# A planner that writes out the order of a fused attention and FFN kernel: DMA transposes dearer and limited in the plan, load costs set anew, and a new order for every engine

## The chip, the cores and the metric

The kernel runs on one core of a Trainium2 chip. A core has five engines that run side by side and wait for each other by semaphores: TensorE (PE in the profile; PEld is its weight load), VectorE (DVE), ScalarE (ACT), GpSimd (POOL) and SyncE (SP). The metric is the device time of one execution in microseconds. Three runs of the kernel before took 253.11 to 253.57 us, with a median of 253.48 us.

## The reference, cut to what matters

```python
B, H, S, D = 8, 8, 576, 64               # chunks of 64 positions: 9 in a batch entry, 72 in all
scores = scale * np.matmul(q_c, k_c.transpose(0, 1, 2, 4, 3))
scores = scores - np.max(scores, axis=-1, keepdims=True)
attn = np.exp(scores); attn = attn / (np.sum(attn, axis=-1, keepdims=True) + 1e-09)
out = np.matmul(attn, v_c)
x = out.transpose(0, 2, 1, 3).reshape(B * S, H * D)      # 4608 x 512
a, b = x @ w1, x @ w2                                    # w1, w2: 512 x 1024
y = (a * b @ w3) @ w_out                                 # w3: 1024 x 1024, w_out: 1024 x 512
```

Attention stays within a chunk of 64 positions and one head. All inputs and the output are float32; the kernel computes in bfloat16 with float32 sums.

## The kernel before, in words

**The work.** Two chunks (128 tokens) make a group; there are 36 groups, g0 to g35. Nine FFN tiles take four groups (512 tokens) each. The two last weights are multiplied into one first (`w3o` = w3 times w_out, `add_w3o`, L526).

For a group (`add_group`, L351) the steps are these. GpSimd loads q and k into a tile `raw` and casts them on the way (`load_qk`, L264). The tile is transposed: on TensorE for g0 to g11 (g0 to g3 from `quad` tiles of their own), and for g12 to g35 by a DMA transpose that SyncE issues (`qk_turn`, L409), into a tile `kqT`. Two copies on ACT or DVE (L235, L237) bring the q half into `qd`. TensorE makes the scores `p_sc` (L436; L387 for the quads); in what follows **S(g)** is this step. DVE and ACT make the softmax: maximum, subtraction, exponential, sum, reciprocal, product `an` (L441 to L463). `an` is transposed into `at`: on TensorE for g0 to g15 (L468), and for g16 to g35 by another DMA transpose on SyncE (`at_turn`, L415). TensorE multiplies `at` with `vd`, the loaded v (L479; L394 for the quads); this step is **V(g)**. A copy puts the result into `xt`.

An FFN tile (`add_tile`, L564) makes 8 pairs of blocks of four matmuls from `xt` with w1 and w2 (L576), an ACT copy and a DVE product for each pair (L235, L585), then four blocks of eight matmuls with `w3o` (L607), and copies their results out. SyncE stores them to `out`; the stores are queued after all loads of q and k.

**Queues.** All loads of q, k, v, w1, w2, w3 and the second half of w_out are issued by GpSimd into one queue (q0 in the profile), in the order of the list `LOADS` (L18) and then g by g. An issue waits for the landing of the load eight places ahead of it, and for a free tile. There are six `raw` tiles; one of g12 or later comes free when its DMA transpose has landed. SyncE's queue (q1) takes the first half of w_out together with ACT's (q10), then the DMA transposes, then the stores. There are four `kqT` tiles, six `at` tiles and three `vd` tiles (`BUFS`, L203). SyncE issues in order: an instruction that waits holds up all that are behind it.

**The order.** No loop nest sets the order. `Plan.run` (L70) simulates the five engines and the two DMA queues with a cost for every operation, and takes on each free engine the ready operation with the lowest key; the keys tell how far ahead of their use attention steps are to be made (`AHEAD`, L31). The sequence in which operations start in this simulation is the order in which they are emitted (L659 to L672), and so the order of each engine's instructions. The plan's times do not reach the chip in any other way, except through `fills`: where the plan sees TensorE idle early on, it puts in matmuls on zeros (L670) that nobody reads, one for each 0.25 us of the gap. In the plan a DMA sits in a ring; a transpose of q and k costs 1.75 us of the 16 DMA engines (L498) and one of `an` costs 0.88 us (L515). Both are counted as landed 3.5 us (`lag`) after their transfer is through, and the only limit on a ring is that it holds eight.

Of the kernel before, what the change touches and what calls it, by code (L numbers as in the profile page):

```python
# [29 lines left out]
LATE, LATE_A = 5, 2  # L30
AHEAD = [31, 28, 25, 19, 16]  # L31


class Op:


    def __init__(self, engines, cost, key, emit, after, takes, uses, lag, issue):
        self.engines = engines if isinstance(engines, tuple) else (engines,)
        self.cost, self.key, self.emit, self.lag, self.issue = cost, key, emit, lag, issue
        self.after, self.takes = list(after), takes  # L40
        self.users = {n: [] for n in takes}
        for taker, n in uses:
            taker.users[n].append(self)
        self.start = self.end = self.engine = None


class Plan:
# [12 lines left out]
    def add(self, engines, cost, key, emit, after=(), takes=(), uses=(), lag=0.1, issue=0.0):  # L60
        o = Op(engines, cost, key, emit, after, takes, uses, lag, issue)
# [8 lines left out]
    def run(self):  # L70
# [13 lines left out]
        rings, flown, reach = {"POOL": [], "SP": []}, 2.2, {"POOL": 1.6, "SP": 1.3}  # L84
# [25 lines left out]
        while left or any(rings.values()):  # L110
# [16 lines left out]
            for eng in free:  # L127
                if free[eng] > now or len(rings.get(eng, ())) + (eng == "POOL" and sum(x > now for x in landed)) >= self.RING:
                    continue
                pick = [o for o in (loads[:1] if eng == "POOL" else todo[eng]) if ready(o)]  # L130
                if not pick:
                    continue
                o = min(pick, key=lambda o: (o.key, o.place))
                for e in o.engines:
                    todo[e].remove(o)
                if eng == "POOL":
                    loads.pop(0)
                o.start, o.engine = now, eng
# [12 lines left out]
                if o.issue:  # L151
                    heapq.heappush(ends, rings[eng][-1][0])
                left -= 1
# [3 lines left out]
            after = ends[:1] + [flown + x[1] * len(h) for x in h]  # L157
            assert after or not left, "the plan is stuck"
# [5 lines left out]
def kernel(  # L164
# [91 lines left out]
    def load(cost, issue, emit, **kw):  # L256
        return plan.add("POOL", cost, 0, emit, lag=landing, issue=issue, **kw)
# [6 lines left out]
    def load_qk(g):  # L264
# [3 lines left out]
        for w, src in enumerate((q, k)):  # L268
            for r, b, c, n in parts:
# [4 lines left out]
                box["ops"].append(load(0.45 * n, 0.5 + 0.2 * n, emit, takes=() if box["ops"] else ("raw",)))  # L274
# [3 lines left out]
    def load_quad(n, y):  # L278
# [4 lines left out]
        for w, src in ((1, k), (0, q)):  # L283
            for t in range(2):
                for c, i0, i1 in parts:
# [8 lines left out]
                    box["ops"].append(load(0.088 * (i1 - i0), 0.5 + 0.02 * (i1 - i0), emit, takes=() if box["ops"] else ("rawq",)))  # L294

    def load_v(b, y0, y1):
        for t in range(2):
# [3 lines left out]
            o = load(1.0 * (y1 - y0), 0.5 + 0.335 * (y1 - y0), emit, takes=() if b in v_first else ("vd",),  # L301
# [5 lines left out]
    def load_w12(j0, j1):  # L307
        for dst, w in ((w1_sb, moe_w1), (w2_sb, moe_w2)):
            for t in range(2):
# [4 lines left out]
                o = load(0.36 * (j1 - j0), 0.62, emit)  # L314
# [10 lines left out]
    def load_wo(k0, k1):  # L325
        def emit(eng):
            nc.gpsimd.dma_start(wo_sb[:, k0:k1, :], moe_w_out.rearrange("(ko p) n -> p ko n", p=P)[:, k0:k1, :])
        wo_got.append([load(0.68 * (k1 - k0), 0.75, emit)])
# [22 lines left out]
    def add_group(g, kt, ks, ka, kv):  # L351
        box = {}
# [161 lines left out]
        if g in A_BY_DMA:  # L514
            ac = plan.add("SP", 0.88, ka, at_turn, after=(an,), takes=("at",), uses=[(an, "an")], lag=3.5, issue=1.3)  # L515
# [114 lines left out]
    made_ident, landing = None, 1.6  # L630
# [72 lines left out]
```

## Time and profile before

| what | value |
|---|---|
| median of three runs | 253.48 us (253.11 to 253.57) |
| the profiled execution, device time | 252.51 us |
| its span, first to last instruction | 250.7 us |
| busy: PE, DVE, ACT, POOL | 240.5, 174.1, 147.5, 100.1 us |
| matmuls, those on zeros included | 1798 |
| loads by GpSimd (q0) | 18.88 MB in 112016 packets |
| transposes and stores by SyncE (q1) | 18.88 MB in 41984 packets |

The profiled execution is 0.97 us below the median of the runs; 1.81 us of its own time lie around the span. A matmul's busy time covers its way through the array, so busy times of matmuls overlap; the distance between the starts of two matmuls tells what one costs. The chain of waits names, piece by piece, what the end of the span waited for; a DMA piece in it runs from the start of its issue to its landing. The timeline gives the start, the length and, in square brackets, the idle time before an instruction and what ended it.

### The profile page before, as it was taken

To read this page: it belongs to the slowest core of one execution; us is meant where nothing else is said; L and a number is where in the kernel's file an instruction comes from. 1 tells how busy PE (TensorE), PEld (TensorE's weight loads), DVE (VectorE), ACT (ScalarE), POOL (GpSimd) and SP (SyncE) were. 2 spreads that over 40 slices of the span, in tenths; PEclk is the share of its full clock that TensorE was granted. 3 is DMA by queue.
4 is the path that set the end of the run, shared out by engine and by line. 5 is a ranking of instruction groups with operands and counts; after the bars stand their busy time and mean duration, and the time that the engine had idled before them with its cause. 6 is when DMAs were issued, how large, how long until landed. Compare 5 with 4: busy or idle time off the path is not lost.

```text
span 250.7 us, 4768 instructions
## 1 busy us (share of the span) xinstructions
PE 240.5 (96%) x1798; PEld 122.3 (49%) x1798; DVE 174.1 (69%) x315; ACT 147.5 (59%) x250; POOL 100.1 (40%) x127
## 2 busy tenths in 40 slices
PE   7599999999999998999999989999999999999995
PEld 2356565456555454454444535454454444444443
DVE  6287879979879795988867978887898842222310
ACT  8666776667766786576558267655666433433222
POOL 8658579976695175357314631820000000000000
PEclk9999999999999999999999999999999999999999
DMA  7999999999999999999999999999999992121114
GB/s 200 173 205 174 175 180 175 166 145 126 135 113 144 150 155 137 139 138 149 133 154 156 136 156 156 142 156 152 137 171 256 388 356 106 43 84 42 44 42 167
DMA packets 154310, 38.58 MB, mean 154 GB/s; under 512 B 141232, under 2 KB 148272, under 8 KB 154288
## 3 DMA queue, kind: packets, MB, share of 16 engines
q0 software_dynamic: 112016, 18.88, 115.5%
q1 hardware_dynamic: 41984, 18.88, 43.2%
q10 hardware_dynamic: 288, 0.52, 0.5%
q8 instruction: 14, 0.23, 0.4%
q14 instruction: 8, 0.07, 0.1%
HBM read 38.80 MB, written 9.44 MB: 192 GB/s over the span
## 4 chain that ended last, share of the span: by engine, by line
PE 54%; DMA 32%; POOL 7%; issue 2%; ACT 2%; POOLq 0%
PE ffn L576 30%; PE ffn L607 20%; DMA kqT<-raw 16%; DMA w_sb<-in_moe_w_dram 10%; DMA raw<-in_k_dram 3%; DMA vd<-in_v_dram 3%; POOL w_sb L311 3%; PE p_av L479 2%; PE p_sc L436 2%; POOL raw L273 2%; ACT qd L235 2%; POOL rawq L292 1%; POOL vd L299 1%; PE ffn L407 1%; ACT rawq L235 0%
## 5 line engine op out<-in xcount | busy, mean ns | idle before, releaser
L576 PE MATMUL ffn<-xt,w_sb 128*128 128x512 bf16 x576 | 134.3, 379 | 0.0
L576 PEld LDWEIGHTS <-w_sb 128*128 128x128 bf16 x576 | 53.7, 98 | 58.2
L585 DVE TENSOR_TENSOR abT<-a_sb,ffn 128x512 bf16<-128x512 f32 x72 | 48.7, 679 | 35.1 <-PE ffn L576 33.1
L607 PE MATMUL ffn<-w3o_sb,abT 128*128 128x512 bf16 (+2 forms) x304 | 67.6, 368 | 0.0
L235 ACT COPY a_sb<-ffn 128x512 f32<-128x512 f32 x72 | 42.0, 583 | 29.5 <-PE ffn L576 27.9
L607 PEld LDWEIGHTS <-abT 128*128 128x128 bf16 x304 | 28.0, 98 | 29.7
L273 POOL DMA_DIRECT2D raw<-in_q_dram x36 | 30.5, 849 | 30.0 <-DMA vd<-in_v_dram 12.6
L273 POOL DMA_DIRECT2D raw<-in_k_dram x36 | 30.5, 851 | 26.3 <-DMA vd<-in_v_dram 15.6
L235 ACT COPY qd<-kqT 64x512 bf16<-64x512 bf16 x37 | 22.8, 615 | 16.4 <-DMA kqT<-raw 16.1
L441 DVE TENSOR_REDUCE nm<-p_sc 128x8 f32<-128x512 f32 x36 | 24.3, 674 | 5.1 <-PE p_sc L436 3.4
L457 DVE TENSOR_REDUCE ss<-e 128x8 f32<-128x520 bf16 x36 | 24.7, 687 | 4.3 <-ACT e L453 3.9
L235 ACT COPY o_sb<-ffn 128x512 f32<-128x512 f32 (+2 forms) x19 | 10.3, 540 | 28.8 <-PE ffn L607 28.8
L453 ACT ACTIVATE e<-sd 128x512 bf16<-128x512 f32 x36 | 22.8, 635 | 4.3 <-DVE sd L449 2.8
L463 DVE TENSOR_TENSOR an<-e,rs 128x512 bf16<-128x512 bf16 x36 | 24.6, 684 | 0.2
L449 DVE TENSOR_TENSOR sd<-p_sc,nm 128x512 f32<-128x512 f32 x32 | 21.8, 681 | 0.4
L299 POOL DMA_DIRECT2D vd<-in_v_dram x16 | 18.5, 1164 | 3.6 <-PE ffn L607 1.4
L235 ACT CAST xt<-p_av 128x512 bf16<-128x512 f32 x25 | 14.6, 585 | 8.1 <-PE p_av L479 6.8
L543 PE MATMUL ffn<-wo_sb,w3t 128*128 128x512 bf16 x64 | 16.3, 380 | 0.3 <-ACT w3t L235 0.2
L479 PEld LDWEIGHTS <-vd 128*128 128x128 bf16 x256 | 11.5, 98 | 8.5 <-DMA at<-an 1.4
L436 PEld LDWEIGHTS <-qd 128*128 128x128 bf16 x256 | 10.6, 98 | 7.5 <-ACT qd L235 3.8
L479 PE MATMUL p_av<-at,vd 128*128 128x64 bf16 x256 | 12.9, 193 | 0.6 <-DMA at<-an 0.3
L237 DVE CAST xt<-p_av 128x512 bf16<-128x512 f32 x11 | 7.6, 691 | 5.8 <-PE p_av L479 5.5
(55 smaller groups left out, 164.9 us busy)
## 6 DMA issues: line engine op xcount, KB each, us to landing
out_dram<-o_sb SPq DMA_DIRECT2D x19, 256.0 KB, 2.3
vd<-in_v_dram POOLq DMA_DIRECT2D x16, 288.0 KB, 13.8
raw<-in_q_dram POOLq DMA_DIRECT2D x28, 128.0 KB, 11.5
raw<-in_k_dram POOLq DMA_DIRECT2D x28, 128.0 KB, 10.4
w_sb<-in_moe_w_dram POOLq DMA_DIRECT2D x8, 256.0 KB, 8.2
w_sb<-in_moe_w_dram POOLq DMA_DIRECT2D x16, 128.0 KB, 5.1
out_dram<-w_sb SPq DMA_DIRECT2D x8, 256.0 KB, 4.0
out_dram<-wo_sb SPq DMA_DIRECT2D x4, 256.0 KB, 4.1
```

What stands on the lines that cost most here:

```text
L235: nc.scalar.copy(o, i)
L273: nc.gpsimd.dma_start(box["t"][r, w], src[b, :, c * C:(c + n) * C, :].rearrange("h p d -> p h d"))
L299: nc.gpsimd.dma_start(vds[b % len(vds)][halves[t], 2 * y0:2 * y1, :, t * D:(t + 1) * D].rearrange("p m c d -> p (m c) d"), v[b, NM * t + 2 ...
L441: nc.vector.tensor_reduce(nm[:, :, 0], box["sc"], axis=AX.X, op=ALU.max)
L449: nc.vector.tensor_sub(sd[:], box["sc"], box["nm"].to_broadcast([P, 8, C]))
L453: nc.scalar.activation(e[:, :, :C], box["sd"][:], ACT.Exp, scale=scale)
L457: nc.vector.reduce_sum(ss[:], box["e"][:], axis=AX.X)
L463: nc.vector.tensor_mul(an[:], box["e"][:, :, :C], box["rs"].to_broadcast([P, 8, C]))
L479: nc.tensor.matmul(t[:, m, cc, :], vds[b % len(vds)][:, m, c, :], box["at"][:, 2 * cc + y, u * C:(u + 1) * C], start=True, stop=True)
L576: nc.tensor.matmul(t[:, :w], wt[:, ki, j * P:(j + 1) * P], x[:, ki, :], start=(ki == 0), stop=(ki == KO - 1))
L585: nc.vector.tensor_mul(box["abT"][:, j, :w], box["as", j][:, :w], box["b", j][:, :w])
L607: nc.tensor.matmul(t[:, :x1 - x0], box["abT"][:, ki, tk * P:(tk + 1) * P], w3o_sb[:, ki, x0:x1], start=(ki == 0), stop=(ki == FO - 1))
```

## The change

The cost model inside the planner is changed, the head of the list of loads is put into another order, and with that the emitted order changes on all engines. No operation of the computation is added, dropped or reshaped.

- SyncE's queue is limited in the plan by the packets that it still holds (`queued`, `QUEUED`), with 2 units for a transpose of q and k, 1 for one of `an` and 0.25 for a store. At over 3.4 units the plan lets SyncE issue nothing.
- The transposes cost 2.0 and 0.95 us instead of 1.75 and 0.88, reach the queue 0.7 us later, and land 1.2 us instead of 3.5 us after their transfer.
- The DMA engines begin 3.5 us into the plan instead of 2.2, and the costs of all loads are set anew.
- In `LOADS` the identity matrix is made after the first quad and two slices of w3; the slices of w3 come in another order; the loads of g6 and g5 change places, as do slices of w1 and w2; v of batch entry 1 comes ahead of g8.

```diff
-LOADS = [('ident',), ('quad', 0, 0), ('w3', 4, 5), ('wo', 4, 8), ('w3', 2, 3), ('w3', 7, 8), ('quad', 0, 1), ('w3', 6,
-         7), ('qk', 4), ('w3', 1, 2), ('w3', 5, 6), ('v', 0, 0, 2), ('w3', 0, 1), ('w3', 3, 4), ('qk', 5), ('w12', 0,
-         2), ('qk', 6), ('w12', 2, 4), ('qk', 7), ('w12', 4, 6), ('w12', 6, 8), ('qk', 8), ('v', 1, 0, 2), ('qk', 9),
+LOADS = [('quad', 0, 0), ('w3', 5, 6), ('w3', 6, 7), ('ident',), ('wo', 4, 8), ('w3', 1, 2), ('quad', 0, 1), ('w3', 4,
+         5), ('w3', 0, 1), ('w3', 2, 3), ('v', 0, 0, 2), ('qk', 4), ('w3', 7, 8), ('w3', 3, 4), ('qk', 6), ('qk', 5),
+         ('w12', 0, 2), ('w12', 2, 4), ('w12', 6, 8), ('qk', 7), ('w12', 4, 6), ('v', 1, 0, 2), ('qk', 8), ('qk', 9),
          ('qk', 10)]
...
+FLOWN, QUEUED, LAG = 3.5, 3.4, 1.2
...
-        rings, flown, reach = {"POOL": [], "SP": []}, 2.2, {"POOL": 1.6, "SP": 1.3}
+        rings, flown, reach = {"POOL": [], "SP": []}, FLOWN, {"POOL": 1.6, "SP": 1.3}
...
+        def queued():
+            return sum(o.units * x / c for _, x, o, c in rings["SP"])
...
+                if eng == "SP" and queued() > QUEUED:
+                    continue
...
-                    rings[eng].append([free[eng] + reach[eng], cost, o])
+                    rings[eng].append([free[eng] + reach[eng] + o.reach, cost, o, cost])
...
-                box["ops"].append(load(0.45 * n, 0.5 + 0.2 * n, emit, takes=() if box["ops"] else ("raw",)))
+                box["ops"].append(load(0.445 * n, 0.5 + 0.2 * n, emit, takes=() if box["ops"] else ("raw",)))
...
-            o = load(1.0 * (y1 - y0), 0.5 + 0.335 * (y1 - y0), emit, takes=() if b in v_first else ("vd",),
+            o = load(1.07 * (y1 - y0), 0.5 + 0.335 * (y1 - y0), emit, takes=() if b in v_first else ("vd",),
...
-        o = load(1.42 * (k1 - k0), 0.75, emit)
+        o = load(1.29 * (k1 - k0), 0.75, emit)
...
-            tr = kc = plan.add("SP", 1.75, kt, qk_turn, after=got, takes=("kqT",), uses=[(got[0], "raw")], lag=3.5, issue=1.3)
+            tr = kc = plan.add("SP", 2.0, kt, qk_turn, after=got, takes=("kqT",), uses=[(got[0], "raw")],
+                               lag=LAG, issue=1.25, units=2, reach=0.7)
...
-            ac = plan.add("SP", 0.88, ka, at_turn, after=(an,), takes=("at",), uses=[(an, "an")], lag=3.5, issue=1.3)
+            ac = plan.add("SP", 0.95, ka, at_turn, after=(an,), takes=("at",), uses=[(an, "an")], lag=LAG, issue=1.25, units=1,
+                          reach=0.7)
...
-    made_ident, landing = None, 1.6
+    made_ident, landing = None, 1.1
```

More of the change, by code (lines that the diff above doesn't have):

```diff
@@ L30, with __init__ @@
 LATE, LATE_A = 5, 2
+FLOWN, QUEUED, LAG = 3.5, 3.4, 1.2
 AHEAD = [31, 28, 25, 19, 16]
 class Op:
-    def __init__(self, engines, cost, key, emit, after, takes, uses, lag, issue):
+    def __init__(self, engines, cost, key, emit, after, takes, uses, lag, issue, units, reach):
         self.engines = engines if isinstance(engines, tuple) else (engines,)
         self.cost, self.key, self.emit, self.lag, self.issue = cost, key, emit, lag, issue
+        self.units, self.reach = units, reach
         self.after, self.takes = list(after), takes
@@ L58, in __init__, with add @@
         self.turn = {n: [] for n in in_turn}
-    def add(self, engines, cost, key, emit, after=(), takes=(), uses=(), lag=0.1, issue=0.0):
-        o = Op(engines, cost, key, emit, after, takes, uses, lag, issue)
+    def add(self, engines, cost, key, emit, after=(), takes=(), uses=(), lag=0.1, issue=0.0, units=0.25,
+            reach=0.0):
+        o = Op(engines, cost, key, emit, after, takes, uses, lag, issue, units, reach)
         self.ops.append(o)
@@ L157, in run @@
             after = ends[:1] + [flown + x[1] * len(h) for x in h]
+            if queued() > QUEUED and rings["SP"][0] in h:
+                x = rings["SP"][0]
+                after.append(flown + min(x[1], (queued() - QUEUED) * x[3] / x[2].units) * len(h) + 1e-6)
             assert after or not left, "the plan is stuck"
@@ L293, in emit @@
                                             src[b, h:h + 2, c * C:(c + i1 - i0) * C, :].rearrange("h (p r) d -> p h (r d)", r=R))
-                    box["ops"].append(load(0.088 * (i1 - i0), 0.5 + 0.02 * (i1 - i0), emit, takes=() if box["ops"] else ("rawq",)))
+                    box["ops"].append(load(0.084 * (i1 - i0), 0.5 + 0.02 * (i1 - i0), emit, takes=() if box["ops"] else ("rawq",)))
     def load_v(b, y0, y1):
```

4 lines of the change are left out of this document (2 added, 2 removed).

## The prediction, as put on record

> **What bounds the kernel now.** I read the page first, then the busy time by stretches, the waits of PE, the chain of waits, and the timelines around the waits.
>
> ```profile
> span 250.7 us, 4768 instructions
> ...
> PE 240.5 (96%) x1798; PEld 122.3 (49%) x1798; DVE 174.1 (69%) x315; ACT 147.5 (59%) x250; POOL 100.1 (40%) x127
> ...
> PE   7599999999999998999999989999999999999995
> ...
> DMA  7999999999999999999999999999999992121114
> ```
>
> PE is busy all the way; only the first two slices and the last show much idle time. The DMA engines are just as full, but only up to about 205 us. So PE's own work is the floor, and what can be gained or lost is the time in which PE waits for a DMA.
>
> ```profile
> 150.93 0.23 PE p_av L479 x8
> 151.17 0.23 PE p_sc L436 x8
> 151.40 4.32 PE ffn L576 x20
> ...
> 56.56 0.45 PE ffn L407 x8
> ```
>
> These pieces of the chain of waits price a matmul from start to start: 216 ns for 512 columns (4.32 / 20), 56 for 128 (0.45 / 8), 29 for 64 (0.23 / 8). I use them for a bookkeeping. The **place** of an instruction is the sum of these prices over all real matmuls ahead of it in PE's order (the quads' 64 transposes, at 28 ns, stand ahead of all places below in both kernels, and fills on zeros are left out). The whole program sums to 229.74 us, before and after alike. The **lag** of an instruction is its start minus its place. Lag never falls; it rises where PE waits or runs a fill. The end of the span moves with the last lag, one for one.
>
> ```profile
> 37.35 1.03 PE L576 MATMUL ffn<-xt,w_sb 128*128 128x512 bf16 x4
> ...
> 73.85 0.40 PE L436 MATMUL p_sc<-kqT,qd 128*128 128x64 bf16 x8
> ...
> 84.20 0.41 PE L436 MATMUL p_sc<-kqT,qd 128*128 128x64 bf16 x8 [0.17 <-ACT qd L235]
> ...
> 100.06 0.41 PE L436 MATMUL p_sc<-kqT,qd 128*128 128x64 bf16 x8 [0.66 <-ACT qd L235]
> ...
> 127.67 0.41 PE L479 MATMUL p_av<-at,vd 128*128 128x64 bf16 x8 [0.35 <-DMA at<-an]
> ...
> 146.21 0.41 PE L436 MATMUL p_sc<-kqT,qd 128*128 128x64 bf16 x8 [1.19 <-ACT qd L235]
> ```
>
> In PE's order these are the first FFN block and S12, S14, S17, V19, S26. Their places in the kernel before, and so their lags:
>
> ```
>           place before  started  lag     place after
> first FFN    23.54        37.35  13.81      23.53
> S12          59.73        73.85  14.12      58.00
> S14          69.74        84.20  14.46      68.02
> S17          84.77       100.06  15.29      84.77
> V19         111.28       127.67  16.39     110.18
> S26         128.46       146.21  17.75     133.87
> ```
>
> So 13.81 us are lost in the start, 3.94 us at waits between S12 and S26 (0.34 up to S14, 0.83 up to S17, 1.10 up to V19, 1.36 at S26), and after S26 none: the stretch from 146.3 to 184 has PE busy for all of its 37.70 us.
>
> ```profile
> 146.30:184.00 37.70, 37.70 (x279) 18.93 (x279) 31.99 (x59) 24.24 (x43) 9.06 (x10) 1.00 1.76 150
> ```
>
> What PE waited for is in the chain and in ACT's timeline:
>
> ```profile
> 63.87 8.59 DMA raw<-in_k_dram
> 72.47 10.40 DMA kqT<-raw
> ...
> 135.71 9.18 DMA kqT<-raw
> ```
> ```profile
> 72.63 0.61 ACT L235 COPY qd<-kqT 64x512 bf16<-64x512 bf16 x1 [0.44 <-DMA kqT<-raw]
> ...
> 82.90 1.24 ACT L235 COPY qd<-kqT 64x512 bf16<-64x512 bf16 x2 [1.06 <-DMA kqT<-raw]
> ```
>
> S14 shows the pattern: the load of its k lands at 72.46 (63.87 + 8.59), its transpose is issued at 72.47 and lands at 82.87, two copies on ACT follow, and S14 starts at 84.20, 1.3 us after 82.90. S12's transpose landed by 72.63; in the kernel before one copy ran on ACT and one on DVE, and S12 was not held up.
>
> **The change part by part.** The costs, the limit on SyncE's queue and the lags are numbers inside the planner. They cost nothing on the chip; only the order and the fills do.
>
> *Start.* The identity matrix moves behind six loads, so GpSimd's first load is issued at 0.74 instead of 1.45, 0.71 us sooner.
>
> ```profile
> 0.74 0.20 POOL masks.py:197 MEMSET ident<- 128x128 bf16 x1 [0.29 <-POOLq L687]
> ...
> 1.45 1.56 POOL L292 DMA_DIRECT2D rawq<-in_k_dram  x2
> ```
> ```profile
> q1 hardware_dynamic: 265, 0.48, 49.8%
> q10 hardware_dynamic: 250, 0.48, 49.6%
> ```
>
> The second fence is the DMA view from 2.4 to 4.9 us: the two queues that bring w_out fill the engines (99.4%). A load that comes 0.71 us sooner takes its share from them, and the sum of bytes lands no sooner. I take 0 of the 0.71 us for everything later in GpSimd's queue, and keep both ends. [...]
>
> The head of `LOADS` only permutes loads: the set ahead of the transposes of g12 to g14 is the same. The fills go from 22 to 25, 14 of them at the head in both, so three more cost at most 3 x 0.216 = 0.65 us. Places in the start move by up to 6 us, but the first FFN block stands at the same place. All of that is covered by the next wait: whatever the lag is before S12, S12 waits until 15.9 (below). Only a start worse by over 1.8 us would show. The tightest is V4, which needs v of batch entry 1 at place 37.56 instead of 40.19.
>
> ```profile
> 45.81 8.46 DMA vd<-in_v_dram
> ```
> ```profile
> 24.00:54.00 30.00, 29.82 (x275) 16.96 (x273) 26.01 (x49) 20.65 (x35) 24.80 (x33) 1.00 2.14 169
> ```
>
> It landed at 54.27 behind the two loads of g8 (256 KB, 1.5 us at 169 GB/s), which now come behind it: about 52.8, a lag of 15.2, covered. If it came no sooner the lag would be 16.7, an end that I keep.
>
> *S12 and S14, loss.* S12 stands 1.73 us earlier, and both its q copies are now on ACT. With the transpose at 72.63 and 1.3 us of copies it can start at 73.93, a lag of 73.93 - 58.00 = 15.93, against 14.12. S14 can start at 84.20: a lag of 84.20 - 68.02 = **16.18**, against 14.46. This costs 1.72 us.
>
> *S17 to V19, gain.* With lag 16.18, S17 wants to start at 100.95; it could at 100.06. The 0.83 us go. For V17 to V19:
>
> ```profile
> 103.99 0.40 PE L436 MATMUL p_sc<-kqT,qd 128*128 128x64 bf16 x8
> ```
> ```profile
> 109.68 0.68 DVE L463 TENSOR_TENSOR an<-e,rs 128x512 bf16<-128x512 bf16 x1
> ```
> ```profile
> 107.49 2.18 SPq L417 DMA_TRANSPOSE at<-an  x1
> 112.34 1.23 SPq L411 DMA_TRANSPOSE kqT<-raw  x1
> 113.62 1.27 SPq L417 DMA_TRANSPOSE at<-an  x1
> ```
> ```profile
> DMA to landing us min/median/max: 7.3/8.3/8.9
> ```
>
> From S18 to its finished `an` took 6.4 us (103.99 to 110.36), and a transpose of `an` 8.3 (the last row, 100 to 160 us). But `an` of g18, done at 110.36, left only at 113.62, behind the transpose of q and k of g22. The new order puts it ahead, and from there SyncE alternates strictly between the two kinds. V18 wants to start at 104.77 + 16.18 = 120.95; S18 runs at 104.87, `an` is done at 111.3, `at` lands at 119.6: in time by 1.4 us. V19 (126.4) has 2 us. The 1.10 us go; S14's part is in the loss above.
>
> *S26, gain.* It stands 5.41 us later and wants 150.05; its transpose landed at 144.89 (135.71 + 9.18), so it is ready at 146.2. The 1.36 us go. What is late next: from g20 to g28 V stands 17.6 to 19.8 us behind S and needs 6.4 + 8.3 = 14.7; g29 has 15.85, the least while GpSimd's loads run. On SyncE a transpose of g(n+4) now waits behind the `at` of g(n), so four groups need 6.4 + 1.3 + 9.4 + 1.3 = 18.4 us (`an`, issue of `at`, transpose of q and k, copies), and PE gives them 20.9 to 23.7.
>
> ```profile
> DMA to landing us min/median/max: 8.0/9.4/11.1
> ```
>
> *Sum.* Last lag 16.18 instead of 17.75: -1.57 us. For waits at those narrow places I give back 0.3 us, the size of the smaller waits above (0.34 at S14). That makes -1.3 us. The tail (stores behind the last matmul) keeps its order. The profiled execution would go from 252.51 to 251.2 us, and the median of the runs, 0.97 us above it, from 253.48 to **252.2**.
>
> **The rivals.** *A, more gained.* The 0.71 us reach the loads of g12 to g14 after all: S14's lag is 15.47, the end -2.3 us, 251.2. Its far end is that S12 and S14 don't wait at all and the lag of 14.46 stays: -3.3 us, 250.2. For it: the loads wait only for each other. Against: the full engines at 2.4 to 4.9 us.
>
> *B, the waits only move.* An `at` that takes 9 to 10 us instead of 8.3 uses up the 1.2 us of g29 and the 1.4 us of V18. With 1 to 1.5 us of new waits the end is -0.6 to -0.1 us, 252.9 to 253.4. For it: 8.9 us was seen. Against: it takes two such places. [...]
>
> *C, slower: the loads up to g14 land later.* S12 and S14 are tied to GpSimd's queue with no slack, so each us by which the load of g14 comes after 72.46 goes into the end. It decides from 2.1 us (16.18 + 2.1 = 17.75 + 0.5) and costs 0.5 to 2 us there: 254 to 255.5. For it: the mix of loads decides the rate, 169 GB/s in the stretch from 24 to 54 us and 127 from 56 to 64.
>
> ```profile
> 56.00:64.00 8.00, 8.00 (x94) 5.12 (x93) 7.03 (x13) 6.43 (x12) 5.78 (x8) 1.00 4.02 127
> ```
>
> Against: the same loads, and from g8 on in the same order.
>
> **How the numbers follow.** Forecast 0.46 (251.5 to 252.9), A 0.18, B 0.16, C 0.20. A measurement of this kernel can tell about 0.2%, 0.5 us, from no change. Forecast and A make faster 0.64, B is same 0.16, C is slower 0.20. The range from 250.2 to 254.7 takes in A's far end, the 16.7 of V4 and the nearer half of C, and leaves out 0.10 above and next to nothing below.
>
> **What would show it.** Right: PE waits for kqT's copies at S12 (about 1.5 us) and S14, lag 15.9 and 16.2 there, no wait at S17, V16 to V19 and S26, and the same lag to the end. A: S12 starts near 73.2. B: waits for `at` at V18, V19 or V29. C: the first transpose of q and k is issued well after 63.6. Wrong altogether: if the lag at the first FFN block is above 15.9, or if PE waits after 150 us.

## The result, and the profile after

The changed kernel took 249.63 us (median of four runs, 249.33 to 250.11), the kernel before 253.44 us beside it (253.11 to 253.57): a ratio of 0.9854, 95% interval 0.9834 to 0.9873. Forecast were 252.2 us and a range of 250.2 to 254.7. The direction was right; the gain is 3.8 us instead of 1.3, and the time lies 0.6 us below the range.

The profiled execution of the changed kernel took 249.81 us. Its page answers the lines shown of before:

```profile
span 248.0 us, 4765 instructions
...
PE 239.6 (97%) x1801; PEld 123.6 (50%) x1801; DVE 173.8 (70%) x315; ACT 146.3 (59%) x250; POOL 100.0 (40%) x127
...
PE   7699999899999999999999999999999999999994
...
DMA  7999999999999999999999999999469994121114
```

PE does the same work in a span shorter by 2.7 us. The dip in the DMA row (46, from 174 to 186 us) is new: the last load lands at 172.3 us and the first store is issued at 184.1, where before the two stood at 184.3 and 185.7. Where the time went is read from PE's timeline at the places of the prediction. Line numbers are higher by 11 to 13 in the changed kernel: L589 is the FFN block that was L576, L447 the scores (L436), L490 the product with v (L479), L418 the transposes of q and k on PE (L407).

```profile
36.86 1.03 PE L589 MATMUL ffn<-xt,w_sb 128*128 128x512 bf16 x4
...
44.69 0.51 PE L418 MATMUL ffn<-ident,raw 128*128 128x128 bf16 x6 [0.72 <-DMA raw<-in_k_dram]
...
52.63 0.28 PE L490 MATMUL p_av<-at,vd 128*128 128x64 bf16 x4 [0.51 <-DMA vd<-in_v_dram]
...
73.06 0.40 PE L447 MATMUL p_sc<-kqT,qd 128*128 128x64 bf16 x8
...
83.08 0.40 PE L447 MATMUL p_sc<-kqT,qd 128*128 128x64 bf16 x8
...
99.82 0.40 PE L447 MATMUL p_sc<-kqT,qd 128*128 128x64 bf16 x8
...
125.23 0.40 PE L490 MATMUL p_av<-at,vd 128*128 128x64 bf16 x8
...
148.92 0.40 PE L447 MATMUL p_sc<-kqT,qd 128*128 128x64 bf16 x8
```

These are the first FFN block, TX3 (the transposes of g7 on PE), the second half of V4, S12, S14, S17, V19 and S26. With their places (TX3 30.49, half of V4 37.44 + 4 x 0.029 = 37.56, the rest as in the prediction's table) the lags are:

```
            place   started   lag     forecast
first FFN   23.53     36.86   13.33
TX3         30.49     44.69   14.20
V4, half    37.56     52.63   15.07    15.2 (covered)
S12         58.00     73.06   15.06    15.93
S14         68.02     83.08   15.06    16.18
S17         84.77     99.82   15.05    16.18
V19        110.18    125.23   15.05    16.18
S26        133.87    148.92   15.05    16.18
```

After V4 the lag does not rise again: in PE's timeline from 54 to 238 us no row carries an idle time. The two waits left of any weight behind the first FFN block are for the k of g7 and for v of batch entry 1. S12 and S14, forecast to lose 1.72 us, do not wait, and the reason is SyncE's queue and ACT (before first, then the changed kernel):

```profile
63.60 19.31 SPq L411 DMA_TRANSPOSE kqT<-raw  x5
```
```profile
60.22 19.34 SPq L422 DMA_TRANSPOSE kqT<-raw  x5
...
70.93 1.24 ACT L246 COPY qd<-kqT 64x512 bf16<-64x512 bf16 x2
...
80.96 1.25 ACT L246 COPY qd<-kqT 64x512 bf16<-64x512 bf16 x2
```

The first DMA transpose, which waits for the k of g12, is issued 3.38 us sooner. ACT's copies for S12 and S14 end at 72.17 and 82.21, each 0.9 us ahead of its scores. So the loads did land sooner, which the prediction had put at nothing. The stretches from 24 to 54, 56 to 64 and 146.3 to 184 us (columns as in the prediction: length, busy time of PE, PEld, DVE, ACT, POOL, clock, DMA share, GB/s):

```profile
24.00:54.00 30.00, 28.58 (x248) 15.84 (x247) 24.71 (x46) 18.81 (x35) 24.85 (x33) 1.00 2.03 172
56.00:64.00 8.00, 8.00 (x92) 5.03 (x91) 6.92 (x16) 5.46 (x11) 6.50 (x9) 1.00 2.51 151
146.30:184.00 37.70, 37.70 (x273) 18.92 (x272) 31.60 (x56) 22.95 (x41) 7.57 (x8) 1.00 1.45 136
```

The middle row is the clue: 151 GB/s instead of 127 from 56 to 64 us. The DMA share adds up the time of all packets over 16 engines, so it passes 1 where packets overlap; 2.51 instead of 4.02 says that a packet took about half the time (for each byte, 2.51 / 151 against 4.02 / 127). The rate rose by 19% only, so the time of a packet does not set the rate by itself, and which of the two follows from the other is not shown.

### The profile page after: what moved, and what is told of

The parts are those of the page before. It is cut to its first block, busy times and chain, and to the rows that moved or that the text cites. A ratio compares the mean times of both kernels' runs of the same rounds, so it can differ in the third digit from the quotient of the medians.

```text
span 248.0 us, 4765 instructions
## 1 busy us (share of the span) xinstructions
PE 239.6 (97%) x1801; PEld 123.6 (50%) x1801; DVE 173.8 (70%) x315; ACT 146.3 (59%) x250; POOL 100.0 (40%) x127
## 4 chain that ended last, share of the span: by engine, by line
PE 79%; DMA 10%; POOL 7%; issue 1%; DVE 1%; ACT 1%; POOLq 0%
PE ffn L589 45%; PE ffn L620 25%; DMA vd<-in_v_dram 7%; POOL w_sb L322 4%; PE p_av L490 3%; PE p_sc L447 3%; DMA rawq<-in_k_dram 2%; POOL raw L284 2%; POOL vd L310 1%; PE ffn L479 1%; PE p_av L683 1%; PE ffn L418 1%; ACT w3t L246 0%; PE ffn L380 0%; DVE qd L248 0%
## 5 line engine op out<-in xcount | busy, mean ns | idle before, releaser
L589 PE MATMUL ffn<-xt,w_sb 128*128 128x512 bf16 x576 | 134.9, 379 | 0.0
L589 PEld LDWEIGHTS <-w_sb 128*128 128x128 bf16 x576 | 53.7, 98 | 57.6
L246 ACT COPY o_sb<-ffn 128x512 f32<-128x512 f32 (+2 forms) x18 | 9.7, 539 | 22.3 <-PE ffn L620 22.2
L246 ACT COPY qd<-kqT 64x512 bf16<-64x512 bf16 x36 | 22.1, 614 | 0.2
L246 ACT CAST xt<-p_av 128x512 bf16<-128x512 f32 x27 | 15.9, 588 | 9.1 <-PE p_av L490 7.3
L556 PE MATMUL ffn<-wo_sb,w3t 128*128 128x512 bf16 x64 | 15.7, 380 | 0.2
L490 PEld LDWEIGHTS <-vd 128*128 128x128 bf16 x256 | 11.4, 98 | 6.3 <-issue 0.6
L447 PEld LDWEIGHTS <-qd 128*128 128x128 bf16 x256 | 11.2, 98 | 5.7 <-ACT qd L246 0.5
L490 PE MATMUL p_av<-at,vd 128*128 128x64 bf16 x256 | 12.8, 193 | 0.5 <-DMA vd<-in_v_dram 0.5
L248 DVE CAST xt<-p_av 128x512 bf16<-128x512 f32 x9 | 6.2, 689 | 5.9 <-PE p_av L490 5.9
```

What stands on the lines that cost most here:

```text
L246: nc.scalar.copy(o, i)
L490: nc.tensor.matmul(t[:, m, cc, :], vds[b % len(vds)][:, m, c, :], box["at"][:, 2 * cc + y, u * C:(u + 1) * C], start=True, stop=True)
L589: nc.tensor.matmul(t[:, :w], wt[:, ki, j * P:(j + 1) * P], x[:, ki, :], start=(ki == 0), stop=(ki == KO - 1))
```

## The experiments

**Theory 1**: the gain is the sooner landing of the loads of g12 and later, brought by the new list of loads. **Theory 2** (the rival): it is the new order in the middle, made by dearer transposes and the limit on SyncE's queue. All times below are medians, and ratios are to the kernel before on the same chip. (The expectation of the first run below uses the two names otherwise: its theory 2 is that the slow stretch is chance in one execution.)

**The kernel before once more, and two halves of the change.** The first has no edit.

> The kernel before once more, unchanged, for a second profile. In the first one the loads of g12 landed at 62.2 and 63.6 us, 2.8 and 1.4 us after the load ahead of each, where a load of that size otherwise takes 0.9; the first DMA transpose left at 63.60, and S14, S17, V17 to V19 and S26 waited. Theory 1 (the old order of loads makes this slow stretch): it comes again, first transpose at 63 to 64 us, last lag 17.5 to 18.7. Theory 2 (the slow stretch is chance in that execution): the first transpose leaves at 60 to 62 us, and the last lag is 1 us or more lower, or the waits stand elsewhere.

The second has the cost and limit of the transposes alone, on the old list and load costs (the transposes of `an` in the same way, not shown):

```diff
+FLOWN, QUEUED, LAG = 2.2, 3.4, 1.2
...
-            tr = kc = plan.add("SP", 1.75, kt, qk_turn, after=got, takes=("kqT",), uses=[(got[0], "raw")], lag=3.5, issue=1.3)
+            tr = kc = plan.add("SP", 2.0, kt, qk_turn, after=got, takes=("kqT",), uses=[(got[0], "raw")],
+                               lag=LAG, issue=1.25, units=2, reach=0.7)
```

> The dearer and limited transposes alone: list of loads, costs of loads and start of the DMA engines as before. The start and all places up to S11 are those of the kernel before; the places from S12 on are near those of the changed kernel (S14 68.02, V18 104.77, S26 132.78). Theory 1 (the gain is the earlier landing of the loads for g12 to g14, which the new start brings): S14 waits until about 84.2, lag 16.2, and nothing later waits: last lag 16.2, 1.5 us under the kernel before (252.0 us). Theory 2 (the gain is the new middle part, the loads matter little): last lag near 15.0, 249.7 us.

The third is the changed kernel with the transposes costed as before (those of `an` too, not shown) and no limit; the fourth has only the limit taken out (`QUEUED = 1e9`).

```diff
-FLOWN, QUEUED, LAG = 3.5, 3.4, 1.2
+FLOWN, QUEUED, LAG = 3.5, 1e9, 3.5
...
-            tr = kc = plan.add("SP", 2.0, kt, qk_turn, after=got, takes=("kqT",), uses=[(got[0], "raw")],
-                               lag=LAG, issue=1.25, units=2, reach=0.7)
+            tr = kc = plan.add("SP", 1.75, kt, qk_turn, after=got, takes=("kqT",), uses=[(got[0], "raw")],
+                               lag=LAG, issue=1.3, units=2, reach=0.0)
```

> The changed kernel with the transposes costed as before and SyncE's queue not limited: new list of loads and new costs of loads. The start is that of the changed kernel up to S11 (V4 at lag 15.07), the places from S12 on are those of the kernel before (S14 69.74, V18 106.50, S26 128.46). Theory 1: the transposes of g12 to g26 land 3 us sooner than in the kernel before, so S17, V16 to V19 and S26 don't wait, or for less than 0.5 us: last lag 15.1 to 15.6, 249.7 to 250.2 us. Theory 2: the waits at V17 to V19 and S26 come back: last lag 16.5 to 17.5, 251.2 to 252.2 us.

> The changed kernel without the limit on SyncE's queue in the plan; the dearer transposes stay. Up to S21 the order of TensorE is that of the changed kernel; from S22 on scores stand up to 4 us earlier (S24 117.79 for 121.48, S26 133.01 for 133.87) and SyncE's order differs from there. Theory 1: the transposes lead by enough there, last lag 15.0 to 15.3, same time as the changed kernel. Theory 2 (the limit is what takes the waits at S26 away): a wait of over 1 us comes back behind S22, last lag above 16.

Measured: before 252.1 us in the profiled execution and 253.24 over 17 runs (251.19 to 255.37); old start with new middle 251.49, ratio 0.9955 (0.9923 to 0.9988); new start with old middle 249.21, 0.9895 (0.9846 to 0.9944); no limit 249.58, 0.9899 (0.9853 to 0.9945). The last lags are 17.3, 16.8, 15.5 and 14.95. So the transposes' costs and the limit are worth 0.45% on the old start, 1.1 us (0.3 to 1.9 by the interval); on the new one nothing shows (249.21 without them, 249.01 to 249.63 for the changed kernel in three measurements). Theory 1 holds for most of the gain.

The second profiled execution of before surprised: its first transpose was issued at 61.60 instead of 63.60, and its waits had moved. This is what its expectation called for if the slow stretch was chance. So one execution of before does not show what the list of loads does, and the runs below have to. PE's timeline at V18 and SyncE's queue ahead of it:

```profile
112.68 1.24 SPq L411 DMA_TRANSPOSE kqT<-raw  x1
113.97 1.27 SPq L417 DMA_TRANSPOSE at<-an  x1
...
123.81 0.39 PE L479 MATMUL p_av<-at,vd 128*128 128x64 bf16 x8 [2.80 <-DMA at<-an]
```

This is the step that the prediction named, `an` of g18 behind the transpose of q and k of g22, but it cost 2.8 us here, and S14, S17 and S26 did not wait at all. With the old start and the new middle this wait is gone, and what is left behind the start is S14 and S17, as forecast for late loads:

```profile
83.84 0.41 PE L447 MATMUL p_sc<-kqT,qd 128*128 128x64 bf16 x8 [0.97 <-ACT qd L246]
...
100.68 0.41 PE L447 MATMUL p_sc<-kqT,qd 128*128 128x64 bf16 x8 [0.77 <-ACT qd L246]
```

**One exchange of the list, undone and done alone.** v of batch entry 1 ahead of g8, in the kernel before and taken back in the changed one; then the whole list alone with all costs old; and a try at the two waits that the changed kernel has left.

```diff
-         2), ('qk', 6), ('w12', 2, 4), ('qk', 7), ('w12', 4, 6), ('w12', 6, 8), ('qk', 8), ('v', 1, 0, 2), ('qk', 9),
+         2), ('qk', 6), ('w12', 2, 4), ('qk', 7), ('w12', 4, 6), ('w12', 6, 8), ('v', 1, 0, 2), ('qk', 8), ('qk', 9),
```

> The kernel before, with only v of batch entry 1 put ahead of the loads of g8 in the list of loads. Theory 1a: it is this one exchange that makes the loads of g12 land sooner. Then v1 lands near 53.6 us, the second load of g12 near 60.5 and the first DMA transpose is issued near 60.6 (as in the three kernels with the new list: 60.2 to 60.6), and PE's last lag is 15 to 16.5 instead of 17.3 to 17.8; the time is 250.0 to 251.8 us. Theory 1b: the sooner landing comes from the new start (identity matrix, w3, g5 and g6) and not from this exchange. Then the first transpose is issued at 61.6 to 63.6 as in the kernels with the old list, the last lag is 16.8 to 18, and the time is 252 to 253.5 us.

> The changed kernel with only this exchange taken back: the loads of g8 ahead of v of batch entry 1. Theory 1a: v1 lands at 54.2 to 54.8 us, the second load of g12 at 61.6 to 63.6, and the first DMA transpose is issued there; S12 (place 57.14) and S14 (place 68.02) then have to wait for their transposes, and the last lag is 15.3 to 16.2 instead of 15.0: 250.0 to 251.2 us. Theory 1b: the first transpose is issued at 60.2 to 60.6, the only wait after TX3 is V4's (place 39.85, lag below 14.9), and the last lag is at most 14.9: 248.8 to 249.6 us.

> The kernel before with the whole new list of loads, all costs in the plan as before (load costs, landing, transposes, no limit). Theory 1 (the gain is the landing of the loads): first transpose issued at 60.2 to 60.8 us, no wait at S14 and S17, a wait of at most 1 us at S26 (place 125.86, 2.6 us earlier than before), last lag 15.0 to 16.2, time 249.3 to 250.8 us. Theory 2 (the new costs and the order that they make bring it): last lag 17 to 18, time 252 to 253.5 us.

For the last, the plan's `lag` of these two loads is raised:

```diff
+MORE_V, MORE_K = {1: 1.4}, {7: 0.8}
...
-    def load(cost, issue, emit, **kw):
-        return plan.add("POOL", cost, 0, emit, lag=landing, issue=issue, **kw)
+    def load(cost, issue, emit, more=0.0, **kw):
+        return plan.add("POOL", cost, 0, emit, lag=landing + more, issue=issue, **kw)
```

> The changed kernel, in whose plan v of batch entry 1 counts as landed 1.4 us later and the q and k of g7 0.8 us later; the list of loads is the same. V4 then stands at place 39.17 instead of 37.44 and TX3 (the transposes of g7) at 31.35 instead of 30.49. If the two waits that the changed kernel has left (0.88 us at TX3, 0.68 us at V4) are all that lies between its last lag of 15.04 and the 13.33 of its first FFN block, both go and no other comes: last lag 13.3 to 13.8, time 248.0 to 248.6 us. If the loads behind have less room than I think, S12 (place 57.14) or S14 or V18 (15.2 us behind S18) take up what is gained: last lag 14.5 to 15.2, time 249.2 to 249.9 us.

Measured, beside 252.51 for before: 255.92 (ratio 1.0172, 1.0094 to 1.0249), 250.29 (0.9929, 0.9885 to 0.9972), 251.51 (0.9972, 0.9933 to 1.0012), 250.04 (0.9936, 0.9905 to 0.9968). The first transposes were issued at 62.41, 61.00, 60.62 and 61.27. So theory 1a falls: the exchange alone brings no sooner landing, and taking it back hardly loses it (61.00 lies between the two forecasts, and the last lag, 15.5, is that of theory 1a). Alone it makes the kernel slower, since the plan then puts S17 2.6 us earlier (place 82.18) while the loads come as late as before: S17 waited 2.54 us, and the last lag was 19.8. That is rival C's mechanism. The whole list alone gained nothing clear of the noise, where theory 1 expected 249.3 to 250.8 us: its loads came as in the changed kernel, but the plan's order with the old costs brought waits from V18 on (last lag 15.96). The try at the two waits gained nothing either: in its profiled execution, the longest of its ten runs (251.07 us), the loads up to w1 and w2 ended at 48.54 instead of 47.14 us, and S12 and the product with v behind it waited.

**The list in two halves.** The first 14 entries new (to `('w3', 3, 4)`), the rest old, and the other way round; the changed kernel beside them, and once more V4 alone planned later (`MORE_V = {1: 0.7}`).

```diff
-LOADS = [('ident',), ('quad', 0, 0), ('w3', 4, 5), ('wo', 4, 8), ('w3', 2, 3), ('w3', 7, 8), ('quad', 0, 1), ('w3', 6,
-         7), ('qk', 4), ('w3', 1, 2), ('w3', 5, 6), ('v', 0, 0, 2), ('w3', 0, 1), ('w3', 3, 4),
+LOADS = [('quad', 0, 0), ('w3', 5, 6), ('w3', 6, 7), ('ident',), ('wo', 4, 8), ('w3', 1, 2), ('quad', 0, 1), ('w3', 4,
+         5), ('w3', 0, 1), ('w3', 2, 3), ('v', 0, 0, 2), ('qk', 4), ('w3', 7, 8), ('w3', 3, 4),
```

> The changed kernel once more, as the measure for the other three on the same chip. If its waits are really gone and not luck of one execution: first DMA transpose issued at 60.0 to 61.0 us, no wait after V4, last lag 14.8 to 15.6, time 249.2 to 250.2 us.

> The kernel before with only the first 14 entries of the list new (identity matrix later, order of w3, v of entry 0 ahead of g4); the rest of the list and all costs are the old ones. The places of S13 to S29 are those of before within 1.1 us, so this is the purest test of the landing. If the head brings the sooner landing: first transpose issued at 60.2 to 61.0, the last lag 14.3 to 15.5, time 249.5 to 250.8 us. If the rest of the list does (g5 and g6 ahead of w1 and w2, v1 ahead of g8): first transpose at 61.5 to 63.6 us, packets near 60 us at 90 to 100 ns as in before, lag 16.8 to 18, time 252 to 253.5 us.

> The other half: the first 14 entries of the list old, the rest new (g6 and g5 ahead of w1 and w2, g7 ahead of the last slice of them, v1 ahead of g8), all costs old. If the rest of the list brings the sooner landing: first transpose at 60.2 to 61.0, packets near 60 us at 40 to 55 ns. If the head does: 61.5 to 63.6 us, and 90 to 100 ns. Its planned middle order is that of no kernel run so far (S17 at place 83.04, S26 at 127.82, both earlier than in before), so its time says less: 250 to 252 us in the first case, 252.5 to 255 us in the second, in which S17 and S26 wait longer than in before.

> The changed kernel, in whose plan only v of batch entry 1 counts as landed 0.7 us later. V4 moves from place 37.44 to 38.30, V5 to 40.07, and from V6 on every place is that of the changed kernel. If V4's wait (0.68 us) is pure loss with nothing behind it: V4's wait goes, last lag 14.2 to 14.5, time 0.6 to 0.9 us below the changed kernel on the same chip. If S12 and S14 have no room behind it, the lag comes back there: same time as the changed kernel within 0.3 us.

Measured, beside 252.62 for before: changed kernel 249.01 (0.9862, 0.9809 to 0.9915), **head alone 249.14** (0.9865, 0.9802 to 0.9927), tail alone 256.21 (1.0143, 1.0079 to 1.0207), V4 a bit later 248.95 (0.9862, 0.9809 to 0.9914). Last lags: 14.5, 14.6, 21.1 and 14.2. The head alone is the whole gain, with S13 to S29 almost at the places of before and every cost old. It is not the landing alone that differs: V16 stands 2.8 us later than in before, and SyncE takes the transpose of g21 ahead of `an` of g16 instead of behind it. Planning V4 later took its wait away, and no time that shows. The windows from 55 to 60 and 60 to 64 us, tail alone first, then head alone:

```profile
55.00:60.00 5.00, 5.00 (x60) 3.20 (x58) 3.10 (x6) 4.05 (x8) 4.70 (x7) 1.00 3.43 148
60.00:64.00 4.00, 4.00 (x46) 2.53 (x44) 3.65 (x8) 3.42 (x7) 2.41 (x3) 1.00 4.07 121
```
```profile
55.00:60.00 5.00, 5.00 (x56) 3.11 (x54) 3.79 (x8) 3.88 (x8) 4.83 (x6) 1.00 2.43 156
60.00:64.00 4.00, 4.00 (x50) 2.47 (x47) 3.62 (x8) 2.90 (x6) 2.81 (x4) 1.00 3.09 144
```

And V18 in both, with the two transposes in SyncE's queue ahead of it (tail alone, then head alone):

```profile
112.61 1.23 SPq L411 DMA_TRANSPOSE kqT<-raw  x1
113.89 1.43 SPq L417 DMA_TRANSPOSE at<-an  x1
...
124.19 0.39 PE L479 MATMUL p_av<-at,vd 128*128 128x64 bf16 x8 [3.22 <-DMA at<-an]
```
```profile
107.92 1.40 SPq L411 DMA_TRANSPOSE kqT<-raw  x1
109.37 3.16 SPq L417 DMA_TRANSPOSE at<-an  x1
...
121.15 0.40 PE L479 MATMUL p_av<-at,vd 128*128 128x64 bf16 x8
```

In both, `an` of g18 stands behind the transpose of g22. With the head, that transpose is issued 4.7 us sooner, so `an` of g18 leaves 4.5 us sooner, and nothing waits. SyncE's order is the same in both up to the transpose of g26, so that order is not what does it. So the new middle order and the new head cure the same wait, and their gains do not add.

**What in the head does it.** Four kernels, each the kernel before with one list of its own; below is the old head, and then the part of each that differs: the identity matrix alone moved; the new head with the identity matrix first; g4 alone moved behind two slices of w3 and v of entry 0; one slice of w3 alone moved ahead of w_out.

```diff
-LOADS = [('ident',), ('quad', 0, 0), ('w3', 4, 5), ('wo', 4, 8), ('w3', 2, 3), ('w3', 7, 8), ('quad', 0, 1), ('w3', 6,
-         7), ('qk', 4), ('w3', 1, 2), ('w3', 5, 6), ('v', 0, 0, 2), ('w3', 0, 1), ('w3', 3, 4),
...
+LOADS = [('quad', 0, 0), ('w3', 4, 5), ('ident',), ('wo', 4, 8),
...
+LOADS = [('ident',), ('quad', 0, 0), ('w3', 5, 6), ('w3', 6, 7), ('wo', 4, 8), ('w3', 1, 2), ('quad', 0, 1), ('w3', 4,
...
+         7), ('w3', 1, 2), ('w3', 5, 6), ('v', 0, 0, 2), ('qk', 4), ('w3', 0, 1), ('w3', 3, 4),
...
+LOADS = [('ident',), ('quad', 0, 0), ('w3', 4, 5), ('w3', 2, 3), ('wo', 4, 8), ('w3', 7, 8), ('quad', 0, 1), ('w3', 6,
```

> The kernel before with only the identity matrix moved behind the first quad and one slice of w3; PE's order is that of before, matmul by matmul. If the sooner landing is the identity matrix's doing (the loads begin 0.2 us sooner and come before GpSimd's mask work): first DMA transpose at 60.2 to 61.3 us, packets at 60 to 62 us 32 to 60 ns, last lag 14.3 to 15.5, time 249 to 250.5 us. If it is the order of the loads themselves: 61.5 to 63.6 us, 85 to 110 ns, lag 16.8 to 18, 252 to 253.5 us.

> The counterpart: the new order of the first loads, but the identity matrix first, as in before; PE's places are those of the kernel with the new head alone. If the identity matrix's place does it: first transpose at 61.5 to 63.6 us, packets near 60 us at 85 to 110 ns, time 251.5 to 253.5 us. If the order of the loads does it: 60.2 to 61.3 us, 32 to 60 ns, time 249 to 249.8 us as with the whole new head (249.14).

> The kernel before with only the q and k of g4 moved behind two slices of w3 and v of entry 0, as in the new head. If what matters is what stands beside v of entry 0 (a load into 64 partitions at a time) in the queue: first transpose at 60.2 to 61.3, packets near 60 us at 32 to 60 ns. If what matters comes earlier in the queue: 61.5 to 63.6 and 85 to 110 ns. The planned order differs from before (S17 at place 83.90, S21 at 99.35), so the time says less: 249.5 to 251 us in the first case, 252.5 to 256 us in the second.

> The kernel before with only one slice of w3 moved ahead of the second half of w_out, as in the new head. If what matters is the very start of the queue, while the two hardware queues bring the first half of w_out: first transpose at 60.2 to 61.3 us, packets near 60 us at 32 to 60 ns. If not: 61.5 to 63.6 and 85 to 110 ns. The planned order differs here too (S20 to S23 up to 3.5 us later): 249.5 to 251 us in the first case, 252 to 255 us in the second.

Measured, beside 252.76 for before: 253.06 (1.0018, 0.9975 to 1.0061), **248.58** (0.9847, 0.9779 to 0.9914), 249.94 (0.9942, 0.9903 to 0.9981), 253.76 (1.0041, 1.0004 to 1.0079). Neither the identity matrix nor the slice of w3, moved alone, brings a gain or the sooner landing. g4 behind v of entry 0 brings a part: 0.6% (0.2 to 1.0) on a planned order of its own, where the whole head brings 1.1 to 1.5%. Its first transpose, at 61.94, lies outside the 60.2 to 61.3 expected for it, while its packets are as short as expected. Below are all profiled executions; "packets" is the mean duration of a packet of GpSimd's queue, worked out from the trace's packet records, and the last two columns are issue times of DMA transposes.

```
g4 ahead of v of entry 0          packets 56-60  60-63 us   g12      g22
before (two executions)                50, 53      99, 68   63.60, 61.60  112.34, 112.68
identity matrix later                      40          77   63.14   113.85
slice of w3 ahead of w_out                 38          64   62.09   112.12
v1 first alone                             44          90   62.41   112.26
tail alone                                 51          81   62.21   112.61
old start, new middle                      48          84   62.49   112.22
g4 behind v of entry 0
g4 later alone                             32          41   61.94   110.60
head alone                                 32          46   61.23   107.92
head, identity matrix first (two)      32, 33      43, 47   60.75, 59.84  107.84, 107.84
list alone                                 33          46   60.62   109.14
changed kernel (three)             32, 33, 35  39, 41, 51   60.22, 59.93, 60.63  111.47, 110.96, 111.16
new start, old middle                      32          40   60.61   109.53
four others with the new list        32 to 34    39 to 49   60.33 to 61.27  110.44 to 111.38
```

The groups don't overlap in packets or at g22; at g12 they do (61.60 in the second execution of before, 61.94 with g4 later alone). In the changed kernel g22 stands behind `an` of g18, so its issue there says less.

So short packets alone don't bring the loads of g12 in. The trace's landing records show what does: a load ends with 16 semaphore steps (all 121 of GpSimd's do, in the first profile of before and in the changed kernel's) and has landed at the last of them: the transpose of g12 is issued 0.01 to 0.02 us behind it in all six executions below. For the k of g12 (times in us; the last column is the time of one 16 KB packet of another queue, q8 "instruction" in the profile, that starts between 56.6 and 59.2 us):

```
                           8th step  15th    16th    q8 packet
before                       60.85   61.62   63.59     1.54
before, second execution     59.80   60.79   61.58     1.52
tail alone                   60.55   61.63   62.19     1.55
g4 later alone               58.77   60.06   61.92     0.89
head alone                   59.65   61.02   61.21     0.97
changed kernel               58.32   59.66   60.20     0.97
```

Of the 3.39 us between before and the changed kernel, 1.96 come with the 15th step, and 1.43 are one last step that hangs behind in before. With g4 later alone the 15th step comes early too, and one late step of 1.86 us is why its transpose was issued at 61.94. The packet of q8 took 1.37 to 1.56 us in the seven executions of the first group and 0.88 to 0.97 in the thirteen of the second; whether it has to do with the late step, the records don't tell.

The landing of g12 is not the whole way to g22 either. It differs by 0.37 us between the second execution of before (61.58) and the head alone (61.21), yet the k of g22, which releases the transpose of g22 in both, landed at 112.53 and 107.36. The rest of that lead is made behind g12, and how is not shown.

The last two runs put the changed kernel and the one with the lowest time on one chip.

> The changed kernel, as the measure for the next one on the same chip: 249.0 to 249.8 us, last lag 14.5 to 15.1.

> The kernel before with only the order of the first loads new and the identity matrix left first, once more beside the changed kernel. If it is the better one for good: 248.4 to 248.9 us, 0.4 to 1.0 us below the changed kernel on the same chip, last lag 14.2 to 14.4. If 248.58 was the chip: within 0.3 us of the changed kernel.

Measured: 249.50 (0.9887, 0.9844 to 0.9929) and 249.43 (0.989, 0.9843 to 0.9937), beside 252.79. On one chip the two are the same within 0.1 us, so the lower 248.58 was no better kernel; why it came out lower there is open, since before took the same on both chips (252.76 and 252.79). On top of the new order of the first loads, nothing else in the change is worth anything that could be measured here, and no version beats the changed kernel by more than the noise.

## Why the prediction was wrong, point by point

**What bounds the kernel**: right. PE's work is the floor and the waits for DMAs are the rest; the span follows the last lag (17.75 to 15.05 is 2.70 us, and the span fell by 2.7). One slip: of the 3.94 us that it puts between S12 and S26, 0.31 lie ahead of S12 (14.12 less 13.81). And it took 0.5 us for what a measurement can tell, from three runs within 0.46 us; over 72 further runs the kernel before scatters by several us (last section).

**The start: this step failed.** It said: "The head of `LOADS` only permutes loads: the set ahead of the transposes of g12 to g14 is the same", and so gave the loads no gain. The set is the same, but the time that it takes is not: with the new order the k of g12 landed at 60.20 us, 3.4 sooner than in the profiled execution of before (1.4 sooner than in its second one), and the k of g14, on which S14's lag of 16.18 rests, at 69.17 instead of 72.46. The kernel with the head alone, which has the gain, shows that it is the order of the first loads that counts. A part of the error is that one execution was priced: in the second one of before the k of g14 landed at 70.91. The 0.71 us that it weighed instead were not there, as GpSimd's first load shows (1.25 us, 0.2 sooner than before), and they are beside the point: the identity matrix, put later alone, brought no gain. That a load issued sooner would only take its share from the full engines was an estimate from the 99.4%; no run shows it.

```profile
1.25 1.54 POOL L303 DMA_DIRECT2D rawq<-in_k_dram  x2 [0.81 <-POOLq L700]
```

The prediction had the fact in its hand, 169 GB/s from 24 to 54 us and 127 from 56 to 64, and used it only against the change, in rival C.

**V4**: forecast lag 15.2, measured 15.07. But it was called covered, and it is what sets the last lag in the profiled execution: the cover, S12 and S14, was gone.

**S12 and S14**: the loss of 1.72 us did not come, for the reason above. Where the loads do come late the step is right in kind: with the old start and the new middle S14 waited at a lag of 15.8 (forecast 16.18).

**S17 to V19, and S26**: all these waits went, as forecast. By itself, on the old list, the new middle order brought 1.1 us (0.3 to 1.9), close to the 1.3 that the prediction gave the whole change. But the credit is shared: with the head alone the waits go too, while `an` of g18 still stands behind the transpose of g22 as in before. And they were no fixed sum: the second execution of before had none of them but V18's. So the right direction does not speak for the sum by which it was found.

**The sum.** Last lag 15.05 instead of 16.18, and the 0.3 us given back were not needed: together 1.43 us, about what the profiled execution beat its forecast by (251.2 against 249.81). The rest up to the 2.6 us of the median is the step from one execution to the median: before, the profiled one lay 0.97 us below it, after, 0.18 above. I carried the 0.97 over. Most likely it belonged to before's waits, whose length differs from run to run (between S17 and V19 the lag rose by 1.10 us in the first profiled execution; in the second V18 alone waited 2.80).

**The rivals.** A came, by another way: its far end (S12 and S14 don't wait, 250.2) was the nearest to the result, with the 0.71 us as its cause, which is refuted. B did not come: from 100 to 160 us the transposes of `an` landed 6.6 to 8.6 us after their issue in the changed kernel, median 7.4. C's mechanism is real: the tail alone and v1 first alone are slower by 1.4% and 1.7%, because the plan put steps earlier for loads that came no sooner. In their profiled executions a wait had a second price: behind waits of 3.22 and 2.38 us the granted clock of TensorE fell to half for 3.41 us, and the lag grew by another 1.6 to 1.7 us. The page of the tail alone shows it in two of its 40 slices:

```profile
PEclk9999999999999999999889999999999999999999
```

**Open**: why the packets from 56 to 63 us take longer with g4 ahead of v of entry 0, loads that land by 29.5 us in the first profile of before and by 28.1 in the changed kernel's. One reading is that the order of loads that write 64 partitions and loads that write 128 leaves the 16 parts of the later loads further apart. The records speak against its plain form: the 16 steps of the k of g11 are spread over 1.24 to 2.91 us in the first group and 1.69 to 2.44 in the second. The other reading is that a later coincidence of transfers hangs on small shifts; the one late step and the longer packet of q8 would fit it. The packet records name no engine, and no experiment here looked at this alone. Open too is what the slices of w3 add to g4's place, and how the lead grows up to g22.

## What to carry to other kernels

A permutation of loads keeps their bytes but need not keep their rate or their landing (here 151 GB/s instead of 127 from 56 to 64 us, and the k of g12 at 60.20 us instead of 63.59 and 61.58): before counting it at nothing, look at how the DMA rate and the packets' time change along the span, and take any slow stretch as something that the order may cure. Where several waits without slack lie one behind the other, don't price them from one execution, and don't add the gains of two edits that cure the same one. Before giving credit to a whole change, run its parts on an order of the engines that stays as near to the old one as can be: here 14 entries of a list brought all that could be measured.

## What the runs showed of the hardware

- From 60 to 64 us all queues together ran at 107 to 132 GB/s (DMA share 3.64 to 4.54) in the seven executions with g4 ahead of v of entry 0, and at 140 to 152 GB/s (2.68 to 3.16) in those with it behind (at most 15 GB/s of it SyncE's transposes).
- A load of 128 KB landed with its last of 16 steps 0.02 to 1.96 us behind the 15th (k of g12, 20 executions).
- The lead differs along the queue: with the new head on the old rest (three executions) the first transpose of q and k was issued at 59.8 to 61.2 us instead of 61.6 to 63.6, that of g22 at 107.8 to 107.9 instead of 112.1 to 113.9.
- After waits of TensorE of 3.22 and 2.38 us its clock was granted at half for 3.41 us (from 125.3 us with the tail alone, from 99.4 with v1 first alone); after waits of 2.80 us (second execution of before) and 2.6 us (identity matrix later) it was not.
- Over 72 runs at a mean granted clock above 0.993 the kernel before took 250.18 to 254.72 us; the changed kernel took 248.71 to 250.11 over 14 runs, all at 0.998 or more. That the scatter comes from waits without slack fits this, but was not shown alone.
